# Key tiles of 128 rows by way of HBM, and the last 32 keys' value matmuls in four row groups of the TensorE

One core of one Trainium2 chip. The metric is device time in microseconds (us), the median of several executions; lower is better.

## The reference

A conformer block over `x` of shape (2, 4000, 512): a feed-forward, attention without masking over the 4000 tokens of each batch, a convolution module, a second feed-forward and a layer norm. The part that matters here is the attention, with one head of width 512:

```python
h = _layernorm(x1, axis=-1)
q = h @ w_q
k = h @ w_k
v = h @ w_v
scores = jnp.einsum('btd,bsd->bts', q, k) * scale
p = _softmax(scores, axis=-1)
attn = jnp.einsum('bts,bsd->btd', p, v) @ w_o
x2 = x1 + attn
```

## The kernel before

The kernel folds `w_q` with `w_k` and `w_v` with `w_o`, so keys and values are both the normalized tokens `h`. It keeps a batch's `h` in SBUF twice: `h[kt]` with keys on partitions, for the value matmuls, and `hT` with features on partitions, for the scores. 4000 keys are 32 tiles of 125, each padded with three zero rows. The first batch's tiles are written by the layer norm in SBUF and transposed from there; the second batch's go through HBM and come back tile by tile while the last group of the first batch works.

There are 16 groups of 500 queries. A group runs through all 32 key tiles; per tile it has four score matmuls into one S bank (a bank is a 128x512 buffer in PSUM, where matmuls write), an exponential on ScalarE (ACT) into `P`, an addition to the denominator on VectorE (DVE), and four value matmuls into the four Y banks, which gather over all tiles. Value matmuls come four tiles after their scores. So a group's last value matmuls come behind the fourth score block of the *next* group.

```python
# attention (shortened)
for kt in range(TB):                       # TB = 32 tiles of 125 keys
    ...
    for cc in range(DC):
        self.mm(ps[:, 0:CHUNK], self.hT[kc][:, kj, cc, :], self.qT[s][:, cc, :],
                cc == 0, cc == DC - 1 and not self.any_score, ...)
    self.act(self.P[p], ps[:, 0:CHUNK], AF.Exp, [b_ps], [self.b_P[p]], scale=SCALE)
    ...                                    # acc += P on DVE
    def values(kt=kt, p=p, g=g):
        for dc in range(DC):
            self.mm(self.Yb[dc][:, 0:CHUNK], self.h[kt][:, dc * 128:(dc + 1) * 128], self.P[p],
                    kt == 0, kt == TB - 1, ...)
        if kt == TB - 1:
            self.finish_queries(g, done)   # copies Y0..Y3 out: ACT takes 0 and 2, DVE 1 and 3
    self.lags.append(values)
    if g == 0 and kt < LAG:
        ...
    elif len(self.lags) > LAG:             # LAG = 4
        self.pop(1)
    ...
    hook(g, kt)   # among others: for groups 3 to 16, eight convolution matmuls at kt == 3 and at kt == 8
```

Of the kernel before, what the change touches and what calls it, by code (L numbers as in the profile page):

```python
# [6 lines left out]
BF16 = mybir.dt.bfloat16  # L7
I32 = mybir.dt.int32
ALU = mybir.AluOpType
AF = mybir.ActivationFunctionType  # L10
AX = mybir.AxisListType

B, T, D, F, KW = 2, 4000, 512, 2048, 3
TILE = 125
CHUNK = 500
# [5 lines left out]
TB = T // TILE  # L21
# [197 lines left out]
class Conformer:  # L219
# [19 lines left out]
    def memory(self):  # L239
# [7 lines left out]

        A = Region(nc, "keys", 65536)
        self.h = [A.view(k * 1024, D) for k in range(TB)]
        self.b_h = [A.buf("h%d" % k, k * 1024, 1024) for k in range(TB)]  # L250
        o = TB * 1024
# [145 lines left out]
        self.m3 = C.view(oLT + 4096, CHUNK, parts=3)  # L397
        self.b_m3 = [C.buf("m3", oLT + 4096 + j * 250, 250) for j in range(TPC)]
# [17 lines left out]
        self.keys2 = nc.dram_tensor("keys2", [TB * 128, D], BF16, kind="Internal").ap()  # L416
        self.b_keys2 = [Buf("keys2") for _ in range(TCB)]
# [46 lines left out]
    def mm(self, out, lhsT, rhs, start, stop, reads, bank, inc=None):  # L464
        self.S.op("PE", lambda e: e.matmul(out, lhsT, rhs, start=start, stop=stop),  # L465
                  reads=reads, writes=[bank], inc=stop if inc is None else inc)
# [110 lines left out]
    def ln_job(self, c, at, kind, eng="DVE", gap=1, slot=None):  # L577

        sl = self.nxt("ln", self.LN_SLOTS)

        def tile(ti):
            if kind == "key2":
                self.ln_norm(c, sl, ti, self.h2[ti][0:TILE, :], self.b_h2[ti], eng)
                if ti == TPC - 1:
                    k = c % TCB
                    dst = self.keys2[k * 512:(k + 1) * 512, :].rearrange("(t p) d -> p t d", p=128)
                    self.store(dst, self.h2c, self.b_h2, [self.b_keys2[k]])
                return
            if kind == "key":
                k = c % TCB  # L590
                tok, b_tok = self.h[k * TPC + ti], self.b_h[k * TPC + ti]
                feat, b_feat = self.hT[k][:, ti], self.b_hT[k][ti]
            else:
                s = slot if slot is not None else c % 2
                tok, b_tok = self.ltm[ti], self.b_ltm[ti]
                feat, b_feat = self.lnT[s][:, ti], self.b_lnT[s][ti]
            self.ln_norm(c, sl, ti, tok[0:TILE, :], b_tok, eng)
            self.transpose(feat, tok, [b_tok], [b_feat])

        t = at  # L600
        for ti in range(TPC):
            self.after(t, lambda ti=ti: self.ln_stats(c, sl, ti))
            if ti % 2:
                t += gap
        self.after(t, lambda: self.ln_aggr(c, sl, eng == "ACT"))
        t += 2 * gap
        for ti in range(TPC):
            self.after(t, lambda ti=ti: tile(ti))
            if ti % 2:
                t += gap  # L610
        return t
# [65 lines left out]

    def residual(self, ps, b_ps, g, scalar, b_scalar=()):

        self.S.op("DVE", lambda e: e.scalar_tensor_tensor(  # L680
            out=self.XT[g], in0=ps, scalar=scalar, in1=self.XT[g], op0=ALU.mult, op1=ALU.add),
            reads=[b_ps, self.bx[g]] + list(b_scalar), writes=[self.bx[g]])
# [71 lines left out]
    def q_group(self, b, qc, dc):  # L754

        s = qc % 2
        ps, b_ps = self.sbank()
        out = ps[:, 0:CHUNK].rearrange("p (t k) -> p t k", t=TPC)
        for cc in range(DC):
            self.mm(out, self.M[:, cc, dc * 128:(dc + 1) * 128], self.hT[qc][:, :, cc, 0:TILE],  # L760
                    cc == 0, cc == DC - 1, [self.b_M] + self.b_hT[qc], b_ps)
        if dc % 2:
            self.S.op("DVE", lambda e: e.tensor_copy(self.qT[s][:, dc, :], ps[:, 0:CHUNK]),  # L763
                      reads=[b_ps], writes=[self.b_qT[s][dc]])
        else:
            self.act(self.qT[s][:, dc, :], ps[:, 0:CHUNK], AF.Copy, [b_ps], [self.b_qT[s][dc]])

    def row_max(self, qc):

        S, s = self.S, qc % 2  # L770
        for ti in range(TPC):
            for kc in range(TCB):
                ps, b_ps = self.sbank()
                out = ps[0:TILE, 0:CHUNK].rearrange("p (t k) -> p t k", t=TPC)
                for cc in range(DC):
                    self.mm(out, self.qT[s][:, cc, ti * TILE:(ti + 1) * TILE], self.hT[kc][:, :, cc, 0:TILE],
                            cc == 0, cc == DC - 1, [self.b_qT[s][cc]] + self.b_hT[kc], b_ps)
                S.op("DVE", lambda e, ps=ps, kc=kc: e.tensor_reduce(
                    self.mx[:, kc:kc + 1], ps[0:TILE, 0:CHUNK], AX.X, ALU.max),
                    reads=[b_ps], writes=[self.b_mx[kc]])  # L780
# [22 lines left out]
    def attention(self, old, hook, done):  # L803
        S = self.S
        LAG = 4
        for g in range(NCK):
            b, qc = divmod(g, TCB)
            s = qc % 2
            if self.any_score:
                if qc == 0:  # L810
                    self.pop(len(self.lags))
                    if b:
                        for kt in range(TB):
                            self.second_keys(kt)
                        for dc in range(DC):
                            self.q_group(1, 0, dc)
                self.row_max(qc)
            for kt in range(TB):
                kc, kj = divmod(kt, TPC)
                ps, b_ps = self.sbank()  # L820
                p = self.nxt("P", self.NP)
# [8 lines left out]
                if kt == 0:  # L830
                    S.op("DVE", lambda e, p=p: e.tensor_copy(self.acc[s], self.P[p]),
                         reads=[self.b_P[p]], writes=[self.b_acc[s]])
                else:
                    S.op("DVE", lambda e, p=p: e.tensor_tensor(  # L834
                        out=self.acc[s], in0=self.acc[s], in1=self.P[p], op=ALU.add),
                        reads=[self.b_P[p], self.b_acc[s]], writes=[self.b_acc[s]])

                if kt == TB - 1:
                    self.split_sums(s)
                    if g < NCK - 1:  # L840
                        self.sums_by_query(s)

                def values(kt=kt, p=p, g=g):
                    for dc in range(DC):
                        self.mm(self.Yb[dc][:, 0:CHUNK], self.h[kt][:, dc * 128:(dc + 1) * 128], self.P[p],
                                kt == 0, kt == TB - 1, [self.b_h[kt], self.b_P[p]], self.b_Y[dc],
                                inc=kt == TB - 1 or dc == DC - 1)
                    if kt == TB - 1:
                        self.finish_queries(g, done)
# [6 lines left out]
                if g + 1 < NCK and kt in (14, 16, 18, 20) and not (self.any_score and g + 1 == TCB):  # L856
                    self.q_group((g + 1) // TCB, (g + 1) % TCB, (kt - 14) // 2)
                if not self.any_score:
                    if g == TCB - 1 and kt >= 6:
                        self.second_keys(kt - 6)  # L860
                    if g == TCB and kt < 6:
                        self.second_keys(TB - 6 + kt)
# [3 lines left out]
    def second_keys(self, kt):  # L866

        kc, kj = divmod(kt, TPC)
        src = self.keys2[kt * 128:(kt + 1) * 128, :]
        self.load(self.h[kt], src, [self.b_h[kt]], reads=[self.b_keys2[kc]])  # L870
        self.transpose(self.hT[kc][:, kj], src, [self.b_keys2[kc]], [self.b_hT[kc][kj]])
# [10 lines left out]
    def sums_by_query(self, s):  # L882
# [5 lines left out]
        def reduce():  # L888
            S.op("DVE", lambda e: e.tensor_reduce(
                self.sq[s], self.sT[0:TILE, :, :, 0:TILE].rearrange("p h c k -> p c h k"), AX.XY, ALU.add),  # L890
# [278 lines left out]
    def constants(self):  # L1169
# [4 lines left out]
        for j in range(TPC):  # L1174
# [6 lines left out]

        S.op("POOL", lambda e: e.memset(self.onec, 1.0), writes=[self.b_onec])
        S.op("POOL", lambda e: e.affine_select(
            out=self.onec, in_=self.onec, pattern=[[0, 2]], compare_op=ALU.is_ge, fill=0.0,
            base=TILE - 1, channel_multiplier=-1), reads=[self.b_onec], writes=[self.b_onec])
        S.op("POOL", lambda e: e.memset(self.one3, 0.0), writes=[self.b_one3])
        S.op("POOL", lambda e: e.memset(self.one3[:, 0:TILE], 1.0), reads=[self.b_one3], writes=[self.b_one3])

    def zero_keys(self, kc):
        for k in range(kc * TPC, (kc + 1) * TPC):  # L1190
            self.S.op("POOL", lambda e, k=k: e.memset(self.h[k], 0.0), writes=[self.b_h[k]])


    def program(self, any_score):
# [26 lines left out]
        def ff1(c, old):  # L1221
            def hook(f):
# [4 lines left out]
                if c < TCB and f == 6:  # L1227
                    self.zero_keys(c)
# [5 lines left out]
                if c == TCB - 1 and f < TPC:  # L1234
                    self.S.op("POOL", lambda e: e.memset(self.h2[f], 0.0), writes=[self.b_h2[f]])

            self.ff_chunk(c, old, hook, lambda: self.ln_job(c, 5, "key" if c < TCB else "key2"))
# [225 lines left out]
```

## Time and profile before

| | before |
|---|---|
| median, 4 runs | 2060.54 us (2060.18 to 2060.61) |
| span in the trace | 2056.5 us |
| TensorE (PE) busy | 2044.2 us, 9653 matmuls |
| DVE, ACT, GpSimd (POOL) busy | 1110, 744, 129 us |
| DMA engines, queue 1 | 17.4% of the span |

PE is the bound. Since its busy time is modelled from pipelined matmuls, read the *starts* of matmuls and not their lengths.

### The profile page before, as it was taken

How to read it: one execution, taken by the hardware profiler on the slowest of the kernel's cores; microseconds unless marked ns; L12 is line 12 of the kernel's file. 1: busy time of each engine (PE TensorE's matmuls, PEld its weight loads, DVE VectorE, ACT ScalarE, POOL GpSimd, SP SyncE). 2: the span in 40 equal slices, each digit the busy share in tenths (PEclk: the TensorE clock that was granted, in tenths of full speed). 3: DMA queues.
4: the chain of work that ended last, by engine and by line, in shares of the span. 5: the costliest groups of instructions: out<-in, count | busy, mean ns of one | idle time of the engine just before them, and what ended most of it. 6: DMA issues, size and time to landing. Idle time of an engine off the chain costs nothing.

```text
span 2056.5 us, 24392 instructions
## 1 busy us (share of the span) xinstructions
PE 2044.2 (99%) x9653; PEld 1037.7 (50%) x9653; DVE 1110.0 (54%) x2274; ACT 744.3 (36%) x1270; POOL 128.7 (6%) x275
## 2 busy tenths in 40 slices
PE   9999999999999999999999999999999999999998
PEld 5555555554444444444444444444445555555554
DVE  4244444325556667666666676667764443443443
ACT  3433333333333333333333333333345443443432
POOL 2012100000000000000000000000011000000000
PEclk9999999999999999999999999999999999999999
DMA  7232221110001100114301010101143111111111
GB/s 181 54 62 57 56 61 49 46 49 11 16 6 24 24 16 18 21 23 110 92 17 24 18 24 14 23 18 24 38 129 93 31 31 41 31 31 41 31 31 42
DMA packets 209324, 87.73 MB, mean 43 GB/s; under 512 B 157873, under 2 KB 208692, under 8 KB 209204
## 3 DMA queue, kind: packets, MB, share of 16 engines
q1 hardware_dynamic: 208808, 85.79, 17.4%
q8 instruction: 78, 1.28, 0.3%
q14 instruction: 42, 0.34, 0.1%
q10 hardware_dynamic: 396, 0.31, 0.0%
HBM read 29.53 MB, written 19.04 MB: 24 GB/s over the span
## 4 chain that ended last, share of the span: by engine, by line
PE 98%; DVE 1%; issue 0%; POOL 0%; DMA 0%; SPq 0%; ACT 0%; POOLq 0%; DVEq 0%; ACTq 0%
PE s L465 55%; PE y L465 42%; DVE wff L1062 0%; DVE work L547 0%; DMA wff<-in_w_ff_a_dram 0%; DVE xt L680 0%; SPq L519 0%; DVE work L569 0%; POOL work L674 0%; POOL work L1071 0%; DVE wff L967 0%; DVE work L504 0%; ACT work L507 0%; PE y L493 0%; DVE work L1069 0%
## 5 line engine op out<-in xcount | busy, mean ns | idle before, releaser
L507 ACT ACTIVATE work<-s 128x500 bf16<-128x500 f32 (+1 forms) x1060 | 621.6, 587 | 1219.8 <-PE s L465 1218.2
L465 PE MATMUL s<-work,wff 128*128 128x500 bf16 (+2 forms) x2592 | 628.3, 373 | 2.5 <-DVE work L504 1.7
L465 PE MATMUL s<-work,keys 128*128 128x500 bf16 x2048 | 517.5, 374 | 0.1
L465 PE MATMUL y<-work,keys 128*128 128x500 bf16 x2048 | 514.4, 373 | 0.1
L465 PE MATMUL y<-wff,work 128*125 128x512 bf16 x2016 | 506.6, 379 | 0.0
L834 DVE TENSOR_TENSOR work<-work 128x500 f32<-128x500 f32 x496 | 334.4, 674 | 282.1 <-ACT work L507 279.2
L465 PEld LDWEIGHTS s<-work,wff 128*128 128x128 bf16 x2592 | 251.9, 98 | 280.3 <-issue 2.1
L465 PEld LDWEIGHTS y<-wff,work 128*125 128x125 bf16 x2016 | 275.2, 137 | 173.5
L465 PEld LDWEIGHTS y<-work,keys 128*128 128x128 bf16 x2048 | 199.2, 97 | 234.4 <-DVE work L899 1.1
L465 PEld LDWEIGHTS s<-work,keys 128*128 128x128 bf16 x2048 | 199.8, 98 | 232.2 <-DVE work L763 0.6
L680 DVE SCALAR_TENSOR_TENSOR xt<-y,xt 125x512 bf16<-125x512 f32 x128 | 79.7, 683 | 343.8 <-PE y L465 343.8
L547 DVE BATCH_NORM_STATS2 work<-xt 125x6 f32<-125x512 bf16 x316 | 199.7, 680 | 7.9 <-DMA xt<-in_x_dram 7.7
L556 POOL TENSOR_TENSOR work<-work 125x4 f32<-125x4 f32 x76 | 77.0, 1013 | 1115.2 <-DVE work L554 1115.2
L465 PE MATMUL s<-work 128*125 128x512 bf16 (+3 forms) x524 | 133.5, 379 | 2.1 <-DVE work L1172 1.3
L569 DVE TENSOR_SCALAR work<-xt,work 125x512 bf16<-125x512 bf16 x279 | 111.7, 444 | 16.8 <-POOL work L556 13.0
L680 DVE SCALAR_TENSOR_TENSOR xt<-s,xt 125x512 bf16<-125x512 f32 x56 | 38.7, 692 | 146.4 <-PE s L465 146.4
L465 PEld LDWEIGHTS s<-work 128*125 128x125 bf16 (+2 forms) x524 | 70.3, 136 | 47.9 <-issue 3.5
L680 DVE SCALAR_TENSOR_TENSOR xt<-s,work,xt 125x512 bf16<-125x512 f32 x64 | 48.0, 751 | 32.6 <-PE s L465 32.0
L465 PE MATMUL s<-keys,work 128*128 128x500 bf16 x256 | 64.4, 376 | 0.0
L971 DVE SCALAR_TENSOR_TENSOR wff<-wff,s 128x500 bf16<-128x500 f32 x57 | 38.6, 678 | 43.5 <-PE s L465 41.5
L507 ACT ACTIVATE wff<-s 128x500 f32<-128x500 f32 x67 | 39.2, 586 | 57.2 <-PE s L465 55.2
L507 ACT ACTIVATE work<-keys,work 128x500 bf16<-128x500 bf16 x64 | 50.4, 794 | 1.1 <-DVE work L1076 1.1
(89 smaller groups left out, 493.8 us busy)
## 6 DMA issues: line engine op xcount, KB each, us to landing
xt<-in_x_dram SPq DMA_DIRECT2D x15, 500.0 KB
out_dram<-work SPq DMA_DIRECT2D x15, 500.0 KB
dcvd<-wff SPq DMA_DIRECT2D x52, 125.0 KB, 1.7
keys<-dcvd SPq DMA_DIRECT2D x13, 500.0 KB, 4.4
wff<-in_w_ff_a_dram SPq DMA_DIRECT2D x16, 256.0 KB, 4.4
keys<-work SPq DMA_DIRECT2D x8, 512.0 KB, 3.6
keys<-keys SPq DMA_DIRECT2D x32, 128.0 KB, 2.1
work<-work SPq DMA_TRANSPOSE x210, 2.5
```

The source lines that it names most:

```text
L465: self.S.op("PE", lambda e: e.matmul(out, lhsT, rhs, start=start, stop=stop), reads=reads, writes=[bank], inc=stop if inc is None else inc)
L507: return self.S.op("ACT", lambda e: e.activation(out, in_, func, **kw), reads=reads, writes=writes)
L547: self.S.op("DVE", lambda e: e.bn_stats(self.st[sl][:, ti, :], x), reads=[b_x], writes=[self.b_st[sl][ti]])
L556: S.op("POOL", lambda e: e.tensor_tensor(out=self.rs[sl], in0=self.va[sl], in1=self.neghalf[0:TILE, :], op=ALU.pow), reads=self.b_va[sl] + ...
L569: self.S.op("DVE", lambda e: e.tensor_scalar(out, x, self.mv[sl][:, ti, 0:1], self.rs[sl][:, ti:ti + 1], ALU.subtract, ALU.mult), reads=[b ...
L680: self.S.op("DVE", lambda e: e.scalar_tensor_tensor(out=self.XT[g], in0=ps, scalar=scalar, in1=self.XT[g], op0=ALU.mult, op1=ALU.add), rea ...
L834: S.op("DVE", lambda e, p=p: e.tensor_tensor(out=self.acc[s], in0=self.acc[s], in1=self.P[p], op=ALU.add), reads=[self.b_P[p], self.b_acc[ ...
L971: self.S.op("DVE", lambda e: e.scalar_tensor_tensor(out=out, in0=self.th[k], scalar=1.0, in1=ps[:, 0:CHUNK], op0=ALU.add, op1=ALU.mult), r ...
```

## The change

Its intent: cut the keys into 31 tiles of 128 and one of 32, and use the array that the small tile leaves idle. The 32 keys are stored four times in the last tile, so that scores and exponentials come out in four copies, one in each quarter of the partitions. The four value matmuls of that tile then take one copy each, on four different row groups of the array and into four different banks, and can run at once. Tiles of 128 don't fit the chunks of 125 x 4 tokens in which the layer norm makes them, so both batches now go through HBM, and the queries, which used to be read from `hT`, get their own transposes. The core of the diff, shortened:

```diff
-TB = T // TILE
+KT = -(-T // 128)
+REST = T % 128
...
+    def store_keys(self, c):                      # 500 rows to HBM; at a batch's end also the tail, four times
...
+            S.dma("SP", k, *[lambda e, r=r: e.dma_start(self.tailsd[b, r:r + REST, :],
+                                                        self.h2[TPC - 1][TILE - REST:TILE, :])
+                             for r in range(0, 128, REST)], ...)
...
+    def fetch_queries(self, b, qc, ti):
+        self.transpose(self.lnT[sl][:, ti], self.keysd[b, t0:t0 + 128, :], ...)
...
                 def values(kt=kt, p=p, g=g):
                     for dc in range(DC):
-                        self.mm(self.Yb[dc][:, 0:CHUNK], self.h[kt][:, dc * 128:(dc + 1) * 128], self.P[p],
-                                kt == 0, kt == TB - 1, [self.b_h[kt], self.b_P[p]], self.b_Y[dc],
-                                inc=kt == TB - 1 or dc == DC - 1)
+                        r = slice(dc * REST, (dc + 1) * REST) if kt == KT - 1 else slice(0, 128)
+                        self.mm(self.Yb[dc][:, 0:CHUNK], self.h[kt][r, dc * 128:(dc + 1) * 128], self.P[p][r],
+                                kt == 0, kt == KT - 1, [self.b_h[kt], self.b_P[p]], self.b_Y[dc],
+                                inc=kt == KT - 1 or dc == DC - 1,
+                                **({"tile_position": (dc * REST, 0)} if kt == KT - 1 else {}))
...
+                if g + 1 < NCK and 7 <= kt < 7 + TPC:
+                    self.fetch_queries((g + 1) // TCB, (g + 1) % TCB, kt - 7)
...
+                if c > TCB and f >= 2 and f % 2 == 0:        # first batch's keys, during chunks 9 to 13
+                    k = (c - TCB - 1) * 7 + f // 2 - 1
+                    if k < KT:
+                        self.key_tile(0, k)
...
-    def zero_keys(self, kc):
```

More of the change, by code (lines that the diff above doesn't have):

```diff
@@ L248, in memory @@
         A = Region(nc, "keys", 65536)
-        self.h = [A.view(k * 1024, D) for k in range(TB)]
-        self.b_h = [A.buf("h%d" % k, k * 1024, 1024) for k in range(TB)]
-        o = TB * 1024
+        self.h = [A.view(k * 1024, D) for k in range(KT)]
+        self.b_h = [A.buf("h%d" % k, k * 1024, 1024) for k in range(KT)]
+        o = KT * 1024
         self.hT = [A.view(o + t * 4096, 2048).rearrange("p (t c k) -> p t c k", t=TPC, c=DC)
@@ L396, in memory @@
         self.b_one3 = Buf("one3")
-        self.m3 = C.view(oLT + 4096, CHUNK, parts=3)
-        self.b_m3 = [C.buf("m3", oLT + 4096 + j * 250, 250) for j in range(TPC)]
+        self.m3 = C.view(oP + (self.NP - 1) * 1024, CHUNK, parts=3)
+        self.b_m3 = [C.buf("m3", oP + (self.NP - 1) * 1024 + j * 250, 250) for j in range(TPC)]
         self.hl = C.view(oHL, 1024).rearrange("p (h c k) -> p h c k", h=2, c=DC)
@@ L415, in memory @@
         self.b_Y = [Buf("y%d" % i, excl=True) for i in range(4)]
-        self.keys2 = nc.dram_tensor("keys2", [TB * 128, D], BF16, kind="Internal").ap()
-        self.b_keys2 = [Buf("keys2") for _ in range(TCB)]
+        self.keysd = nc.dram_tensor("keysd", [B, KT * 128, D], BF16, kind="Internal").ap()
+        self.b_keysd = [Buf("keysd") for _ in range(NCK)]
+        self.tailsd = nc.dram_tensor("tailsd", [B, 128, D], BF16, kind="Internal").ap()
+        self.b_tailsd = [Buf("tailsd") for _ in range(B)]
         self.dcvd = nc.dram_tensor("dcvd", [self.NBESIDE, 128, DC * CHUNK], BF16, kind="Internal").ap()
@@ L461, in drain, with mm @@
             self.tick()
-    def mm(self, out, lhsT, rhs, start, stop, reads, bank, inc=None):
-        self.S.op("PE", lambda e: e.matmul(out, lhsT, rhs, start=start, stop=stop),
+    def mm(self, out, lhsT, rhs, start, stop, reads, bank, inc=None, **kw):
+        self.S.op("PE", lambda e: e.matmul(out, lhsT, rhs, start=start, stop=stop, **kw),
                   reads=reads, writes=[bank], inc=stop if inc is None else inc)
@@ L581, in tile @@
         def tile(ti):
-            if kind == "key2":
+            if kind == "key":
                 self.ln_norm(c, sl, ti, self.h2[ti][0:TILE, :], self.b_h2[ti], eng)
                 if ti == TPC - 1:
-                    k = c % TCB
-                    dst = self.keys2[k * 512:(k + 1) * 512, :].rearrange("(t p) d -> p t d", p=128)
-                    self.store(dst, self.h2c, self.b_h2, [self.b_keys2[k]])
+                    self.store_keys(c)
                 return
-            if kind == "key":
-                k = c % TCB
-                tok, b_tok = self.h[k * TPC + ti], self.b_h[k * TPC + ti]
-                feat, b_feat = self.hT[k][:, ti], self.b_hT[k][ti]
-            else:
-                s = slot if slot is not None else c % 2
-                tok, b_tok = self.ltm[ti], self.b_ltm[ti]
-                feat, b_feat = self.lnT[s][:, ti], self.b_lnT[s][ti]
+            s = slot if slot is not None else c % 2
+            tok, b_tok = self.ltm[ti], self.b_ltm[ti]
+            feat, b_feat = self.lnT[s][:, ti], self.b_lnT[s][ti]
             self.ln_norm(c, sl, ti, tok[0:TILE, :], b_tok, eng)
@@ L676, in ln_factor @@
              reads=[self.b_va[sl][ti], self.b_neghalf], writes=[self.b_rs[sl][ti]])
+    def store_keys(self, c):
+        b, qc = divmod(c, TCB)
+        S, dst = self.S, self.keysd[b, qc * CHUNK:(qc + 1) * CHUNK, :].rearrange("(t p) d -> p t d", p=TILE)
+        k = S.dsems[36 + self.nxt("st", 8)]
+        S.dma("SP", k, *[lambda e, lo=lo, hi=hi: e.dma_start(dst[lo:hi], self.h2c[lo:hi]) for lo, hi in self.ROWS],
+              reads=self.b_h2, writes=[self.b_keysd[c]])
+        if qc == TCB - 1:
+            n = 128 - TILE
+            self.store(self.keysd[b, T:T + n, :], self.h2[TPC - 1][TILE:128, :], [self.b_h2[TPC - 1]],
+                       [self.b_keysd[c]])
+            k = S.dsems[36 + self.nxt("st", 8)]
+            S.dma("SP", k, *[lambda e, r=r: e.dma_start(self.tailsd[b, r:r + REST, :],
+                                                        self.h2[TPC - 1][TILE - REST:TILE, :])
+                             for r in range(0, 128, REST)],
+                  reads=[self.b_h2[TPC - 1]], writes=[self.b_tailsd[b]])
     def residual(self, ps, b_ps, g, scalar, b_scalar=()):
@@ L754, in q_group @@
     def q_group(self, b, qc, dc):
-        s = qc % 2
+        s, sl = qc % 2, 1 if b or qc else 0
         ps, b_ps = self.sbank()
@@ L759, in q_group @@
         for cc in range(DC):
-            self.mm(out, self.M[:, cc, dc * 128:(dc + 1) * 128], self.hT[qc][:, :, cc, 0:TILE],
-                    cc == 0, cc == DC - 1, [self.b_M] + self.b_hT[qc], b_ps)
+            self.mm(out, self.M[:, cc, dc * 128:(dc + 1) * 128], self.lnT[sl][:, :, cc, 0:TILE],
+                    cc == 0, cc == DC - 1, [self.b_M] + self.b_lnT[sl], b_ps)
         if dc % 2:
@@ L766, in q_group @@
             self.act(self.qT[s][:, dc, :], ps[:, 0:CHUNK], AF.Copy, [b_ps], [self.b_qT[s][dc]])
+    def fetch_queries(self, b, qc, ti):
+        sl, t0 = 1 if b or qc else 0, qc * CHUNK + ti * TILE
+        self.transpose(self.lnT[sl][:, ti], self.keysd[b, t0:t0 + 128, :],
+                       self.b_keysd[b * TCB + qc:b * TCB + min(qc + 2, TCB)], [self.b_lnT[sl][ti]])
     def row_max(self, qc):
@@ L773, in row_max @@
                 ps, b_ps = self.sbank()
-                out = ps[0:TILE, 0:CHUNK].rearrange("p (t k) -> p t k", t=TPC)
+                out = ps[0:TILE, :].rearrange("p (t k) -> p t k", t=TPC)
                 for cc in range(DC):
-                    self.mm(out, self.qT[s][:, cc, ti * TILE:(ti + 1) * TILE], self.hT[kc][:, :, cc, 0:TILE],
+                    self.mm(out, self.qT[s][:, cc, ti * TILE:(ti + 1) * TILE], self.hT[kc][:, :, cc, :],
                             cc == 0, cc == DC - 1, [self.b_qT[s][cc]] + self.b_hT[kc], b_ps)
                 S.op("DVE", lambda e, ps=ps, kc=kc: e.tensor_reduce(
-                    self.mx[:, kc:kc + 1], ps[0:TILE, 0:CHUNK], AX.X, ALU.max),
+                    self.mx[:, kc:kc + 1], ps[0:TILE, :], AX.X, ALU.max),
                     reads=[b_ps], writes=[self.b_mx[kc]])
@@ L812, in attention @@
                     if b:
-                        for kt in range(TB):
-                            self.second_keys(kt)
-                        for dc in range(DC):
-                            self.q_group(1, 0, dc)
+                        for kt in range(KT):
+                            self.key_tile(1, kt)
                 self.row_max(qc)
-            for kt in range(TB):
+            for kt in range(KT):
                 kc, kj = divmod(kt, TPC)
                 ps, b_ps = self.sbank()
-                p = self.nxt("P", self.NP)
+                p = self.nxt("Pa", self.NP - 1) if self.any_score else self.nxt("P", self.NP)
                 for cc in range(DC):
@@ L833, in attention @@
                 else:
-                    S.op("DVE", lambda e, p=p: e.tensor_tensor(
-                        out=self.acc[s], in0=self.acc[s], in1=self.P[p], op=ALU.add),
+                    n = REST if kt == KT - 1 else 128
+                    acc = self.acc[s][0:n]
+                    S.op("DVE", lambda e, p=p, n=n, acc=acc: e.tensor_tensor(
+                        out=acc, in0=acc, in1=self.P[p][0:n], op=ALU.add),
                         reads=[self.b_P[p], self.b_acc[s]], writes=[self.b_acc[s]])
-                if kt == TB - 1:
+                if kt == KT - 1:
                     self.split_sums(s)
@@ L844, in values @@
                     for dc in range(DC):
-                        self.mm(self.Yb[dc][:, 0:CHUNK], self.h[kt][:, dc * 128:(dc + 1) * 128], self.P[p],
-                                kt == 0, kt == TB - 1, [self.b_h[kt], self.b_P[p]], self.b_Y[dc],
-                                inc=kt == TB - 1 or dc == DC - 1)
-                    if kt == TB - 1:
+                        r = slice(dc * REST, (dc + 1) * REST) if kt == KT - 1 else slice(0, 128)
[3 more added lines that the diff above has]
+                                **({"tile_position": (dc * REST, 0)} if kt == KT - 1 else {}))
+                    if kt == KT - 1:
                         self.finish_queries(g, done)
@@ L855, in attention @@
                     self.pop(1)
-                if g + 1 < NCK and kt in (14, 16, 18, 20) and not (self.any_score and g + 1 == TCB):
+                if g + 1 < NCK and 7 <= kt < 7 + TPC:
+                    self.fetch_queries((g + 1) // TCB, (g + 1) % TCB, kt - 7)
+                if g + 1 < NCK and kt in (14, 16, 18, 20):
                     self.q_group((g + 1) // TCB, (g + 1) % TCB, (kt - 14) // 2)
@@ L859, in attention, with key_tile @@
                     if g == TCB - 1 and kt >= 6:
-                        self.second_keys(kt - 6)
+                        self.key_tile(1, kt - 6)
                     if g == TCB and kt < 6:
-                        self.second_keys(TB - 6 + kt)
+                        self.key_tile(1, KT - 6 + kt)
                 hook(g, kt)
                 self.tick()
-    def second_keys(self, kt):
+    def key_tile(self, b, kt):
         kc, kj = divmod(kt, TPC)
-        src = self.keys2[kt * 128:(kt + 1) * 128, :]
-        self.load(self.h[kt], src, [self.b_h[kt]], reads=[self.b_keys2[kc]])
-        self.transpose(self.hT[kc][:, kj], src, [self.b_keys2[kc]], [self.b_hT[kc][kj]])
+        if kt == KT - 1:
+            src, rd = self.tailsd[b], [self.b_tailsd[b]]
+        else:
+            src = self.keysd[b, kt * 128:(kt + 1) * 128, :]
+            lo, hi = kt * 128 // CHUNK, (kt * 128 + 127) // CHUNK
+            rd = self.b_keysd[b * TCB + lo:b * TCB + hi + 1]
+        self.load(self.h[kt], src, [self.b_h[kt]], reads=rd)
+        self.transpose(self.hT[kc][:, kj], src, rd, [self.b_hT[kc][kj]])
     def split_sums(self, s):
@@ L889, in reduce @@
             S.op("DVE", lambda e: e.tensor_reduce(
-                self.sq[s], self.sT[0:TILE, :, :, 0:TILE].rearrange("p h c k -> p c h k"), AX.XY, ALU.add),
+                self.sq[s], self.sT[0:TILE].rearrange("p h c k -> p c h k"), AX.XY, ALU.add),
                 reads=self.b_sT, writes=[self.b_sq[s]])
@@ L1182, in constants @@
         S.op("POOL", lambda e: e.memset(self.onec, 1.0), writes=[self.b_onec])
-        S.op("POOL", lambda e: e.affine_select(
-            out=self.onec, in_=self.onec, pattern=[[0, 2]], compare_op=ALU.is_ge, fill=0.0,
-            base=TILE - 1, channel_multiplier=-1), reads=[self.b_onec], writes=[self.b_onec])
-        S.op("POOL", lambda e: e.memset(self.one3, 0.0), writes=[self.b_one3])
-        S.op("POOL", lambda e: e.memset(self.one3[:, 0:TILE], 1.0), reads=[self.b_one3], writes=[self.b_one3])
-    def zero_keys(self, kc):
-        for k in range(kc * TPC, (kc + 1) * TPC):
-            self.S.op("POOL", lambda e, k=k: e.memset(self.h[k], 0.0), writes=[self.b_h[k]])
+        S.op("POOL", lambda e: e.memset(self.one3, 1.0), writes=[self.b_one3])
     def program(self, any_score):
@@ L1226, in hook @@
                     self.ln_job(c + 1, 1, "in")
-                if c < TCB and f == 6:
-                    self.zero_keys(c)
                 if c == 0 and f == 8:
@@ L1233, in hook @@
                     self.after(6, self.taps)
-                if c == TCB - 1 and f < TPC:
+                if c > TCB and f >= 2 and f % 2 == 0:
+                    k = (c - TCB - 1) * 7 + f // 2 - 1
+                    if k < KT:
+                        self.key_tile(0, k)
+                if c == NCK - 1 and f >= FC - TPC:
+                    self.fetch_queries(0, 0, f - FC + TPC)
+                if c == 0 and f < TPC:
                     self.S.op("POOL", lambda e: e.memset(self.h2[f], 0.0), writes=[self.b_h2[f]])
-            self.ff_chunk(c, old, hook, lambda: self.ln_job(c, 5, "key" if c < TCB else "key2"))
+            self.ff_chunk(c, old, hook, lambda: self.ln_job(c, 5, "key"))
         old = 0
```

## The prediction

> **What bounds the kernel now.** I read the page first: busy time, then the chain that ended last.
>
> ```profile
> span 2056.5 us, 24392 instructions
> PE 2044.2 (99%) x9653; PEld 1037.7 (50%) x9653; DVE 1110.0 (54%) x2274; ACT 744.3 (36%) x1270; POOL 128.7 (6%) x275
> ...
> PE 98%; DVE 1%; issue 0%; POOL 0%; DMA 0%; SPq 0%; ACT 0%; POOLq 0%; DVEq 0%; ACTq 0%
> ```
>
> The TensorE is 99% busy and 98% of the chain. A busy PE can hide gaps, so next comes the timeline, in the middle of one attention group (500 queries against all keys of a batch). Columns: start in us, length in us, engine, line, operation, how many merged.
>
> ```profile
> 500.40 1.01 PE L465 MATMUL s<-work,keys 128*128 128x500 bf16 x4
> ...
> 501.25 1.00 PE L465 MATMUL y<-work,keys 128*128 128x500 bf16 x4
> ```
>
> Four matmuls start every 0.845 us, so one 500-wide matmul costs 0.845 / 4 = 0.211 us. 9653 x 0.212 = 2046 us, which is the PE's busy time: there is no slack between matmuls in general, and time is the count of matmuls times their spacing. Only two things can move the end: fewer or overlapping matmuls, and new gaps between them. DVE at 54%, ACT at 36% and DMA at a tenth or two matter only where PE waits for them.
>
> **What the Trainium skill says.** (1) "Perfetto Trace Analysis", Tensor Engine Instruction: a matmul's end in the trace is estimated, not observed. The trace agrees: a matmul is shown 0.374 us long, yet starts are 0.211 us apart. I use starts alone. (2) "TensorE: Matmul & The Clock Gate", Part 3: four matmuls of 32 contraction rows in four row groups run at the same time, starts about 4 ns apart, 3.07x measured for 512 columns. No run here shows it yet. (3) "TensorEngine Tiling (Array Packing)", Key Properties: changing the tiling mode drains the TensorE, changing only the tile does not. This the trace of before does show, in an unexpected place: the tap weights are turned by four matmuls of 3 contraction rows, and the score bound by a matmul with one output row; as built, both are instructions for a part of the array (32 rows by 128 columns; 128 by 32), like the new ones. Here they are between full matmuls, and below them, for control, eight matmuls one column wide that stay on the whole array:
>
> ```profile
> 45.13 1.03 PE L465 MATMUL y<-wff,work 128*125 128x512 bf16 x4
> 46.09 0.25 PE L465 MATMUL s<-work 3*128 3x3 bf16 x4
> 46.28 1.02 PE L465 MATMUL s<-work,wff 128*128 128x500 bf16 x4
> ...
> 93.46 1.03 PE L465 MATMUL y<-wff,work 128*125 128x512 bf16 x4
> 94.42 0.19 PE L465 MATMUL s<-work 128*1 128x1 f32 x2
> 94.54 1.02 PE L465 MATMUL s<-work,wff 128*128 128x500 bf16 x4
> ...
> 1524.30 0.80 PE L465 MATMUL y<-work,keys 128*128 128x500 bf16 x3
> 1524.93 0.58 PE L465 MATMUL s<-work 128*125 128x1 bf16 x8
> 1525.37 1.00 PE L465 MATMUL y<-work,keys 128*128 128x500 bf16 x4
> ```
>
> A merged line ends when its last matmul ends, so the last one started at start + length - one matmul's length (0.379 us for 512 columns, 0.374 for 500, 0.163 for 3, 0.164 for 1x1). Into the small mode: 45.13 + 1.03 - 0.38 = 45.78, next start 46.09, 0.31 us; and 93.46 + 1.03 - 0.38 = 94.11, next 94.42, again 0.31. A 512-wide matmul normally holds its successor for 0.216, so the switch costs about 0.095 us. The control: 1524.30 + 0.80 - 0.37 = 1524.73, next 1524.93, 0.20, no penalty. Back out: 46.09 + 0.25 - 0.16 = 46.18, next 46.28; 94.42 + 0.19 - 0.16 = 94.45, next 94.54: 0.09 to 0.10 after a matmul with almost no columns of its own. So I charge 0.095 us per switch, each way. The four 3-row matmuls started (46.18 - 46.09) / 3 = 0.03 us apart.
>
> **The change, part by part.** *The tiles.* Before, 4000 keys are 32 tiles of 125; after, 31 of 128 and one of 32. The count stays 32, so score matmuls (4 per tile), the exponentials and the sums of the denominator keep their number and, but for one addition of 32 rows, their size. Nothing is gained there.
>
> *The last value tile.* This is the whole gain. Its four 128-row matmuls become four 32-row ones on separate rows of the array and separate banks. From the start of the full matmul before them to the start of the full one after them: before, 5 x 0.211 = 1.057 us. After: 0.211 + 0.095 to enter, 3 x 0.03 to start the other three (I take the spacing that this trace shows, not the page's 4 ns), 0.211 for the last to stream, 0.095 to leave: 0.702 us. Saving: 0.355 us for each of 16 query groups, if nothing else stops PE.
>
> *Where something else does.* The four value banks must be copied out before the next group's first value matmuls overwrite them. Shorter matmuls come to that point sooner; the copies do not, since they queue on ACT and DVE behind an exponential and an addition of the new group, whose start depends on its fourth score block and not on the value matmuls. The boundary between the first and second group:
>
> ```profile
> 520.69 1.01 PE L465 MATMUL s<-work,keys 128*128 128x500 bf16 x4
> ...
> 521.32 1.25 DVE L899 CAST work<-y 128x500 bf16<-128x500 f32 x2
> 521.54 1.48 PE L465 MATMUL y<-work,keys 128*128 128x500 bf16 x4
> ...
> 522.63 0.10 PEld L465 LDWEIGHTS y<-work,keys 128*128 128x128 bf16 x1 [0.47 <-DVE work L899]
> ```
>
> The four value matmuls take 1.48 us in place of 1.00: PE already waits for the DVE copies, which end at 522.57. The last cannot start before 522.63 however soon PE arrives, so here the saving is lost: 0. The same boundary between later groups:
>
> ```profile
> 721.07 1.86 PE L465 MATMUL s<-work,wff 128*128 128x500 bf16 x8
> ...
> 721.64 1.26 DVE L899 CAST work<-y 128x500 bf16<-128x500 f32 x2
> ...
> 722.77 1.01 PE L465 MATMUL s<-work,keys 128*128 128x500 bf16 x4
> ...
> 723.62 1.00 PE L465 MATMUL y<-work,keys 128*128 128x500 bf16 x4
> ```
>
> From the third group on, eight matmuls of the convolution stand in between. The copies end at 722.90 and the first value matmul comes at 723.62, the fourth at 724.25. Moved up 0.355 us they start at 723.27 and 723.90: still no wait. After the last group there are also eight such matmuls before the projection reads the copies. So 15 of 16 groups keep it: 15 x 0.355 = 5.3 us.
>
> *The way through HBM.* Now both batches' keys are stored, loaded and transposed from HBM; before, only the second's. Added: 32 more loads of 128 KB, 32 more key transposes in place of 32 from SBUF, 64 transposes for the queries, and small stores for the tail. The view of DMA issues (KB each, median us to landing) has the same operations:
>
> ```profile
> keys<-keys SPq DMA_DIRECT2D x32, 128.0 KB, 2.1
> ...
> keys<-keys SPq DMA_TRANSPOSE x64, 2.7
> ```
>
> The first batch's keys are issued over chunks 9 to 13 of the first feed-forward, whose chunks last 27.4 us, and used after chunk 15. The queries are fetched at key tiles 7 to 10 and used at 14; the last has four tiles of 1.69 us, 6.8 us, against 2.7. The second batch's keys keep their place. The tail stores after the last chunk follow its normalization (ends 476.4), and the copy that overwrites their source comes at about 482.8 (it follows the query matmuls that start at 481.78): 6 us for seven small transfers against one of 2 to 4 us. Cost on PE: 0. *GpSimd* loses 32 clearings of key tiles; it is 6% busy, so 0.
>
> Sum: 2060.5 - 5.3 = 2055.2 us.
>
> **Rivals.** (a) *No drain worth the name*: the pack takes what the skill's 3.07x gives, 4 x 0.211 / 3.07 = 0.275 us (an estimate from that page's ratio); 15 x (0.845 - 0.275) = 8.5 us, 2052.0. Against it: 0.095 us measured at both small-mode places. With the page's 4 ns between starts but the drain as measured, 0.355 + 3 x 0.026 = 0.43 us, 6.5 us in all, 2054.0. (b) *Weights in the open*: weight loads (0.097 us each, of the value tiles) are not hidden in the pack, and the starts are 0.1 us apart; the saving is 0.634 - 0.19 - 0.3 = 0.14 us, 2.2 us in all, 2058.4. For it: the loads of the 3-row matmuls began only with them, at 46.09, not one matmul early as elsewhere. Against: those started 0.03 us apart. (c) *The four do not overlap at all*: two switches are then pure loss, 16 x 0.19 = 3 us, 2063.5. (d) *A late transfer*: one of the fetches or the tail stores holds PE at a group's query matmuls. Each wait of 1 us in 15 groups would be 15 us, 2070; the margins of 4 us speak against it. (e) The copies become the limit at every boundary, as at the first: gain 0, 2060.5. The eight convolution matmuls speak against it.
>
> **Range and chances.** (a) and (b) bracket what I believe: 2052.5 to 2060.0 leaves room for part of (e) on the upper side. Faster by over 2% would need 41 us; all value matmuls of the last tiles together are 16 x 0.845 = 13.5 us: 1%. Slower by over 2% needs waits of 2.8 us in every group: 2%.
>
> **What would show it.** In the timeline of after, at the end of a group: the last full score matmul, 0.31 us later the first 32-row one, three more within 0.1 us, and the next full one 0.3 us after the last. The boundary of the first two groups: value matmuls stretched by about 0.8 in place of 0.48 us, waiting on the DVE copy; from the third on no such wait. PE's waits naming DMA: none in attention. The prediction is wrong if the 32-row starts lie 0.1 or 0.2 us apart, if the switch costs clearly more or less than 0.095 us, or if a wait on a transfer appears ahead of the query or score matmuls.

## The result, and the profile after

The changed kernel takes 2054.41 us (4 runs, 2054.03 to 2054.93), against 2060.54: 6.1 us less. The ratio is 0.9971, 95% interval 0.9954 to 0.9988. Ratios here are the mean time of one kernel's fast runs over that of the other's of the same rounds, so not quite the ratio of the medians quoted. The point predicted was 2055.2, the range 2052.5 to 2060.0.

The page of after, its span and busy times; below it, from the view by shape, the group of the new matmuls (count, busy us, mean ns of one, idle before). PEld is the loading of weights for PE, SPq below the issuing of transfers:

```profile
span 2050.2 us, 24503 instructions
PE 2037.8 (99%) x9653; PEld 1031.8 (50%) x9653; DVE 1099.0 (54%) x2274; ACT 742.7 (36%) x1270; POOL 112.2 (5%) x241
```

```profile
L470 PE MATMUL y<-work,keys 32*128 32x500 bf16 x64 | 6.2, 380 | 0.0
```

PE still executes 9653 matmuls; it is busy for 6.4 us less because 64 of them overlap. Busy time can show overlap; a count cannot. The end of the second group, in the timeline of before and then of after:

```profile
583.84 1.01 PE L465 MATMUL s<-work,keys 128*128 128x500 bf16 x4
...
584.69 1.00 PE L465 MATMUL y<-work,keys 128*128 128x500 bf16 x4
...
585.53 1.86 PE L465 MATMUL s<-work,wff 128*128 128x500 bf16 x8
```

```profile
583.65 1.01 PE L470 MATMUL s<-work,keys 128*128 128x500 bf16 x4
584.59 0.10 PEld L470 LDWEIGHTS y<-work,keys 32*128 32x128 bf16 x4 [0.41 <-issue]
584.60 0.39 PE L470 MATMUL y<-work,keys 32*128 32x500 bf16 x4
...
584.92 1.87 PE L470 MATMUL s<-work,wff 128*128 128x500 bf16 x8
...
585.92 1.25 DVE L929 CAST work<-y 128x500 bf16<-128x500 f32 x2
...
587.48 1.00 PE L470 MATMUL y<-work,keys 128*128 128x500 bf16 x4
```

The last full matmul before the pack starts at 583.65 + 1.01 - 0.37 = 584.29. The pack starts 0.31 us later, as at the tap weights. The four matmuls together last 0.39 us where one lasts 0.38: they start within 0.01 us. The next full matmul comes at 584.92, 0.32 us after the pack's start. From full to full 584.92 - 584.29 = 0.63 us, against 5 x 0.211 = 1.06 before (585.53 - 584.48 in its lines): 0.43 us saved. The DVE copies end at 587.17, and the next value matmuls start at 587.48 without a wait.

The boundary of the first two groups, again before and then after:

```profile
519.00 1.01 PE L465 MATMUL s<-work,keys 128*128 128x500 bf16 x4
...
522.86 1.01 PE L465 MATMUL s<-work,keys 128*128 128x500 bf16 x4
```

```profile
518.81 1.01 PE L470 MATMUL s<-work,keys 128*128 128x500 bf16 x4
...
519.75 0.39 PE L470 MATMUL y<-work,keys 32*128 32x500 bf16 x4
...
520.08 1.02 PE L470 MATMUL s<-work,keys 128*128 128x500 bf16 x4
...
521.04 0.38 PE L470 MATMUL y<-work,keys 128*128 128x500 bf16 x1
521.13 1.26 DVE L929 CAST work<-y 128x500 bf16<-128x500 f32 x2
...
521.86 0.97 PE L470 MATMUL y<-work,keys 128*128 128x500 bf16 x3 [0.44 <-DVE work L929]
...
522.67 1.01 PE L470 MATMUL s<-work,keys 128*128 128x500 bf16 x4
```

The first score block after the stalled value matmuls starts at 522.67; the fourth score block of this group starts at 518.81. That is 3.86 us. Before, the same two starts are at 519.00 and 522.86: also 3.86. This boundary kept nothing. Its value matmuls are stretched by 522.67 - 521.04 - 0.845 = 0.79 us, as forecast (about 0.8).

### The profile page after: what moved, and what is told of

Read it like the earlier page. It is cut to its first block, busy times and chain, and to the rows that moved or that the text cites. A ratio compares the mean times of both kernels' runs of the same rounds, so it can differ in the third digit from the quotient of the medians.

```text
span 2050.2 us, 24503 instructions
## 1 busy us (share of the span) xinstructions
PE 2037.8 (99%) x9653; PEld 1031.8 (50%) x9653; DVE 1099.0 (54%) x2274; ACT 742.7 (36%) x1270; POOL 112.2 (5%) x241
## 4 chain that ended last, share of the span: by engine, by line
PE 98%; DVE 1%; POOL 0%; issue 0%; ACT 0%; DMA 0%; POOLq 0%; SPq 0%; DVEq 0%; ACTq 0%
PE s L470 55%; PE y L470 42%; DVE work L552 0%; POOL work L672 0%; DVE work L574 0%; DVE wff L1092 0%; DVE xt L695 0%; DMA xt<-in_x_dram 0%; DVE work L509 0%; POOL work L1101 0%; DVE work L665 0%; ACT work L512 0%; DVE wff L997 0%; DVE work L618 0%; DVE work L670 0%
## 5 line engine op out<-in xcount | busy, mean ns | idle before, releaser
L470 PE MATMUL y<-work,keys 128*128 128x500 bf16 (+1 forms) x2048 | 504.6, 374 | 0.4 <-DVE work L929 0.4
L854 DVE TENSOR_TENSOR work<-work 128x500 f32<-128x500 f32 (+1 forms) x496 | 334.4, 674 | 280.0 <-ACT work L512 277.2
L470 PEld LDWEIGHTS y<-work,keys 128*128 128x128 bf16 (+1 forms) x2048 | 194.6, 97 | 234.0 <-issue 6.2
L470 PE MATMUL s<-work 128*125 128x512 bf16 (+2 forms) x780 | 197.7, 378 | 2.0 <-DVE work L1202 1.2
L470 PEld LDWEIGHTS s<-work 128*125 128x125 bf16 (+1 forms) x780 | 95.3, 124 | 76.9 <-issue 3.7
L1071 POOL COPY wff<-wff 128x1 bf16<-128x1 bf16 x56 | 10.5, 187 | 635.4 <-DVE wff L1001 633.0
```

What stands on the lines that cost most here:

```text
L470: self.S.op("PE", lambda e: e.matmul(out, lhsT, rhs, start=start, stop=stop, **kw), reads=reads, writes=[bank], inc=stop if inc is None el ...
L854: S.op("DVE", lambda e, p=p, n=n, acc=acc: e.tensor_tensor(out=acc, in0=acc, in1=self.P[p][0:n], op=ALU.add), reads=[self.b_P[p], self.b_a ...
L1071: S.op("POOL", lambda e: e.tensor_copy(self.G[gs][:, jj, 0:1], self.G[gp][:, jj, CHUNK:CHUNK + 1]), reads=[self.b_G[gp][jj]], writes=[self ...
```

## Experiments

Four kernels ran in each of two calls, each call on one chip; the kernel before took 2060.58 us (9 runs) in the first and 2060.28 us (7 runs) in the second. All eight gave the right result.

**after_again**: the changed kernel, no edit, beside the next three.

> The changed kernel as it is, for its size beside the next three on one chip. Theory (15 boundaries keep 0.42 us each, the trace's value, the first keeps none): 6.3 us under the kernel before, ratio 0.9969. Rival (part of the gain is from elsewhere, such as the way through HBM): the same ratio here, told apart by the next two.

Measured: 2054.70 us (5 runs, 2054.15 to 2054.75), ratio 0.9971, interval 0.9957 to 0.9984. The gain is there on this chip too, 5.9 us by medians.

**hbm_only**: HBM and tiles of 128 without the row groups.

```diff
-                        r = slice(dc * REST, (dc + 1) * REST) if kt == KT - 1 else slice(0, 128)
+                        r = slice(0, 128)
...
-                                inc=kt == KT - 1 or dc == DC - 1,
-                                **({"tile_position": (dc * REST, 0)} if kt == KT - 1 else {}))
+                                inc=kt == KT - 1 or dc == DC - 1)
...
+        if kt == KT - 1:
+            for r in range(REST, 128, REST):
+                self.after(12, lambda r=r: self.S.op("DVE", lambda e: e.memset(self.h[kt][r:r + REST], 0.0), ...))
```

> Tiles of 128 by way of HBM, but the last tile's rows 32 to 127 are cleared and its value matmuls are four of 128 rows, one after the other, as before. Theory: all of the gain is the row groups, so this equals the kernel before, within 0.5 us (ratio 1.000). Rival: the way through HBM or the dropped clearings of GpSimd give something by themselves, and this is 1 us or more faster; or it costs something that the row groups cover, and it is 1 us or more slower.

Measured: 2060.94 us (5 runs, 2060.74 to 2061.22), ratio 1.0002, interval 0.9988 to 1.0015. The medians differ by 0.36 us, and the runs of the kernel before alone spread over 1.4: tiling and transfers together change the time by less than the runs scatter. No part of the gain is theirs, so it lies in the four matmuls per group. Their trace does show one small price, 0.38 us of waiting on a transfer (see (d) below).

**serial_rows**: the two mode switches without work side by side.

```diff
-                        r = slice(dc * REST, (dc + 1) * REST) if kt == KT - 1 else slice(0, 128)
+                        r = slice(0, REST) if kt == KT - 1 else slice(0, 128)
...
-                                **({"tile_position": (dc * REST, 0)} if kt == KT - 1 else {}))
+                                **({"tile_position": (0, 0)} if kt == KT - 1 else {}))
```

> The last tile's four value matmuls keep 32 contraction rows but all use rows 0 to 31, so the same two mode switches without work side by side. Theory: four starts 0.21 us apart between two switches of 0.1 us; 15 x 0.2 us = 3 us over the kernel before, 9.4 us over the changed one (about 2063.6). Rival 1 (the gain is from fewer rows per matmul, not from running at once): as fast as the changed kernel, 2054.4. Rival 2 (weights of one row group can't be loaded while it works): starts 0.31 us apart, about 2069.

Measured: 2063.67 us (4 runs, 2063.54 to 2064.28), ratio 1.0015, interval 1.0000 to 1.0031. Its timeline at the end of the second group:

```profile
583.74 1.01 PE L470 MATMUL s<-work,keys 128*128 128x500 bf16 x4
584.67 0.53 PEld L470 LDWEIGHTS y<-work,keys 32*128 32x128 bf16 x4 [0.41 <-issue]
584.68 1.01 PE L470 MATMUL y<-work,keys 32*128 32x500 bf16 x4
585.62 1.88 PE L470 MATMUL s<-work,wff 128*128 128x500 bf16 x8
```

Four matmuls on one row group last 1.01 us, (1.01 - 0.37) / 3 = 0.21 us from start to start, exactly as full ones: a quarter of the contraction rows saves nothing. The weights are loaded beside a running matmul of the same row group: the last load starts at 584.67 + 0.53 - 0.10 = 585.10, the last matmul only at 584.68 + 1.01 - 0.37 = 585.32. From full to full: 583.74 + 1.01 - 0.37 = 584.38 to 585.62, 1.24 us, 0.19 more than without switches. Running at once is the gain; the switches are its price. Both rivals fall.

**late_first**: the first boundary freed from the copies.

```diff
-                elif len(self.lags) > LAG:
-                    self.pop(1)
+                elif len(self.lags) > LAG and not (g == 1 and kt == 4):
+                    self.pop(2 if g == 1 and kt == 10 else 1)
```

> The changed kernel, but in the second group the first value tile is issued one score block later, so that the copies out of the value banks are over by then; the extra tile of lag is made up at tile 10. Theory (this boundary lost its 0.42 us and the 0.48 us that it already waited to the DVE copies): 0.8 us under the changed kernel, about 2053.6, and no PE wait on the copies there. Rival (PE would wait for something else in that place, or the copies only come later too): no difference, 2054.4.

Measured: 2053.51 us (5 runs, 2053.30 to 2054.26), ratio 0.9965, interval 0.9951 to 0.9979. By medians that is 1.2 us under the changed kernel of the same call, of which 0.8 was expected. The profiled run is the slowest, 2054.26; the other four end by 2053.52. The timeline shows the place itself:

```profile
520.17 1.87 PE L470 MATMUL s<-work,keys 128*128 128x500 bf16 x8
...
521.23 1.25 DVE L929 CAST work<-y 128x500 bf16<-128x500 f32 x2
...
521.88 1.05 PE L470 MATMUL y<-work,keys 128*128 128x500 bf16 x4
...
522.76 1.01 PE L470 MATMUL s<-work,keys 128*128 128x500 bf16 x4
```

Two score blocks run while the copies work, and the value matmuls take 1.05 us in place of 1.00, where the changed kernel stretched them over 522.67 - 521.04 = 1.63 us. From the pack's start (519.85 here, 519.75 in the changed kernel) 2.91 us pass until the next score block in both; but here two score blocks and the value matmuls are done by then, there only one and the value matmuls. One block is 0.845 us. Two waits of weight loads on the copies are left (0.19 and 0.35 us), but cost only the 0.05 by which the value matmuls are longer. Up to the second pack the whole block is kept, first after_again, then late_first:

```profile
519.85 0.39 PE L470 MATMUL y<-work,keys 32*128 32x500 bf16 x4
...
584.69 0.39 PE L470 MATMUL y<-work,keys 32*128 32x500 bf16 x4
```

```profile
519.85 0.39 PE L470 MATMUL y<-work,keys 32*128 32x500 bf16 x4
...
583.85 0.39 PE L470 MATMUL y<-work,keys 32*128 32x500 bf16 x4
```

That is 0.84 us, so the theory holds. The profiled run lost as much again at another place, to a transfer; see (d) below. What the medians differ by beyond this, 0.4 us, is not explained. This version has the lowest median of all.

**switch48 and noswitch48**: the switch by itself. Ahead of three score blocks of each group, one matmul of three columns, whose output the block overwrites; with 32 rows in the first, with 128 in the second (`0:128` in place of `0:32`).

```diff
+                if kt in (11, 13, 25) and not self.any_score:
+                    self.mm(ps[:, 0:3], self.ident[0:32, :], self.ident[0:32, 0:3], True, True, [self.b_ident], b_ps, inc=False)
                 for cc in range(DC):
```

> The changed kernel with one matmul of 32 rows and 3 columns put in ahead of three score blocks of each group (48 in all), so two mode switches each and hardly any work. Theory (0.1 us per switch): 48 x 0.2 = 9.6 us over the changed kernel, about 2064. Rival (the switch is nearly free, and the 0.31 us at the tap weights and at the pack is a wait on something else): under 3 us over the changed kernel.

> The control: the same 48 matmuls of 3 columns with all 128 rows, so no switch. Theory: 0.03 to 0.055 us each, as the one-column matmuls of the kernel before, 1.5 to 2.6 us over the changed kernel, about 2056.5. Rival (any narrow matmul among wide ones costs 0.2 us): as slow as the version with switches.

Measured: 2064.42 us (4 runs, 2064.34 to 2064.91) and 2055.29 us (4 runs, 2055.06 to 2055.74), on the same chip. Timelines, switch48 first, at the first such place of the second group (the fifth of the x5 is the added matmul):

```profile
535.20 1.13 PE L470 MATMUL s<-work 128*125 128x512 bf16 x5
536.26 1.02 PE L470 MATMUL s<-work,keys 128*128 128x500 bf16 x4
```

```profile
534.71 1.03 PE L470 MATMUL s<-work 128*125 128x512 bf16 x5
535.60 1.01 PE L470 MATMUL s<-work,keys 128*128 128x500 bf16 x4
```

Four 512-wide matmuls hold PE for 4 x 0.216 = 0.864 us. With the small matmul in another mode the next block starts after 1.06 us, with the same matmul on the whole array after 0.89. Over all, (2064.42 - 2055.29) / 48 = 0.19 us for two switches. The rival that called 0.31 us a wait on something else falls: the same matmul without a switch has no such gap. The control itself cost less than expected: 0.6 us over the changed kernel, not 1.5 to 2.6. It was run at another time.

**moved_before and moved_after**: the eight convolution matmuls taken from between the last and the first value matmuls of neighbouring groups, in both kernels.

```diff
-            if 0 <= g - 2 < tail and kt in (3, 8):
-                pair(g - 2, 2 + (3, 8).index(kt))
+            if 0 <= g - 2 < tail and kt in (4, 8):
+                pair(g - 2, 2 + (4, 8).index(kt))
```

> The kernel before, with the convolution's eight matmuls at the head of groups 3 to 16 one key tile later, behind the first value tile and not in front of it. Theory: each of these 14 boundaries now waits as the first does, 0.48 us; 6.7 us over the kernel before, about 2067. Rival (the copies have slack without them): no change.

> The same move in the changed kernel. Theory: at these boundaries the pack's gain is lost to the copies, as at the first one, so it is nearly as slow as the kernel before with the move: 0.4 us less (only the last group keeps its gain), about 2066.8. Rival (the gain of the pack doesn't depend on what stands behind it): 6.3 us under the kernel before with the move, about 2061.

Measured: 2066.19 us (4 runs, 2066.06 to 2066.39) and 2065.95 us (4 runs, 2065.83 to 2066.21). The change that is worth 6 us in the original order is worth 0.24 us in this one, and both are slower than the kernel before. The waits of PE's weight loads on the DVE copies (us in total, times, longest), first moved_before, then moved_after, then the changed kernel:

```profile
PEld y L465 <- DVE work L899: 15.5, 30, 0.6
```

```profile
PEld y L470 <- DVE work L929: 17.9, 30, 0.7
```

```profile
PEld y L470 <- DVE work L929: 1.2, 2, 0.7
```

Two waits at one boundary have become 30 at 15. The row groups make PE arrive sooner at banks that come free no sooner. The move cost the kernel before 5.9 us, 0.42 per boundary and not 0.48. (The waits in the table total more than what they cost: a weight load normally starts 0.21 us ahead of its matmul.)

## Why the prediction was right

- *PE alone sets the end.* Held: with everything but the row groups in place (hbm_only) the time is that of the kernel before, although the DMA queue's share rose from 17.4% to 21.5% and GpSimd lost 16.5 us of work.
- *The switch costs 0.095 us each way.* Held, and well beyond the two places it was read from: 0.19 us per pair in switch48 against its control, 0.19 in serial_rows. That it could be read from the kernel before, at four forgotten matmuls of 3 rows, is what made the estimate possible.
- *The other three matmuls start 0.03 us apart.* This term was mis-sized. The trace of after has (0.39 - 0.38) / 3 = 0.003 us (its records, finer than these lines, have starts 3 to 4 ns apart). The 3-row matmuls from which 0.03 was taken all use rows 0 to 2 of the array, so one row group; the 4 ns of the Trainium skill ("TensorE: Matmul & The Clock Gate", Part 3) for different row groups was the better value, as the prediction's second estimate under rival (a) had it (0.43 us per group, 2054.0). That one group is the reason for 0.03 is likely, and was not tested by itself; the control noswitch48 fits, where a matmul of 3 columns on all 128 rows also holds PE for 0.89 - 0.864 = 0.03 us.
- *15 of 16 boundaries keep it.* Held. 15 x 0.43 = 6.4 us, against 6.3 us between the two spans and 6.1 us between the medians. The first boundary kept 0.00 us. That the copies are what decides is shown from both sides: late_first frees that boundary, the moved pair takes the gain from the others.
- *Rivals.* (b), weights in the open, is out: weight loads do start only with the pack (PEld idle 0.41 us before them), but the starts are not 0.1 us apart. What the 0.095 us consist of, a drain of the array or these loads in the open (0.10 us each), no run here separates. (c), no overlap, is out by the trace, and its 2063.5 is what serial_rows measured when overlap was made impossible: 2063.67. (e) is the state that moved_after built.
- *(d), a late transfer.* The prediction put the cost of the transfers on PE at 0 and expected no wait on a DMA in attention. That is slightly off. The fetches that it named never hold the query matmuls. But at one place of the eighth group, while the second batch's keys come in, eight convolution matmuls start late. The kernel before, then late_first:

```profile
965.90 1.01 PE L465 MATMUL y<-work,keys 128*128 128x500 bf16 x4
966.75 1.86 PE L465 MATMUL s<-work,wff 128*128 128x500 bf16 x8
```

```profile
962.47 1.00 PE L470 MATMUL y<-work,keys 128*128 128x500 bf16 x4
964.15 1.86 PE L470 MATMUL s<-work,wff 128*128 128x500 bf16 x8 [0.68 <-DMA work<-work]
```

  From the last value matmul's start, 0.21 us pass before the change and 1.05 in late_first, 0.84 too many. It is 0.07 in the trace of after, 0.32 in after_again and 0.38 in hbm_only. The wait named is on transposes (`work<-work`). That the added transfers push these back in the same queue is likely, and was not tested.

  The margin of the tail stores was misread. The prediction gave seven stores 6 us until a copy overwrites their source. In after, the last four are issued at 480.2 to 481.4 and land about 1.6 us later (the view of their line, then the timeline):

```profile
L688 SPq DMA_DIRECT2D tailsd<-work x4: 324/417/421, 480.2 to 481.4; - x4
DMA to landing us min/median/max: 1.5/1.6/1.6
```

```profile
476.22 0.84 SPq L680 DMA_DIRECT2D keysd<-work  x2
...
480.15 1.71 SPq L688 DMA_DIRECT2D tailsd<-work  x4
...
482.70 0.59 ACT L512 ACTIVATE work<-s 128x500 bf16<-128x500 f32 x1 [1.11 <-PE s L470]
...
495.44 0.68 DVE L778 CAST work<-s 128x500 bf16<-128x500 f32 x1 [0.49 <-PE s L470]
```

  So the stores take from 476.2 to 481.4 + 1.6 = 483.0, 6.8 us, longer than the margin and past the copy at 482.70 that the prediction had in mind. Nothing waited, because that copy overwrites only the buffer's first 1000 bytes, which the large store reads. The tail's source lies in bytes 3072 to 4096 (`h2[3]`; `qT[1]` begins at the same address), and only the fourth query copy reaches it, at 495.44. Here the prediction was right by luck.

  The other transfers took what the same operations took before: key loads 2.3 us against 2.1, key transposes 2.8 against 2.7.

## What to carry to other kernels

Packing small matmuls into row groups is worth (n - 1) matmuls less two mode switches, so count the switches first: here they took 0.19 of the 0.42 us of a pack, and a pack of two would, as an estimate from these numbers, have gained almost nothing (0.21 - 0.19). Then ask what stands right behind the pack: the same banks must be emptied before their next use, PE now gets there sooner, and only other work in between turns the saved time into an earlier end. To price something new, look for a small relative of it in the trace that you have.

## What the Trainium skill lacked or had wrong

- "TensorEngine Tiling (Array Packing)", Key Properties, says that a change of tiling mode drains the TensorE, without a cost. Here: 0.095 us per switch, 0.19 us in and out (switch48 less its control, 48 pairs, 9.1 us), and weight loads of the new mode are not issued ahead of it (PEld idle for 0.41 us before the pack's loads).
- "TensorE: Matmul & The Clock Gate", Part 3: starts about 4 ns apart agree (0.003 us). Its 3.07x for four row tiles does not carry over to a pack within a stream of full matmuls: 0.845 us became 0.63 - 0.21 = 0.42 us, twice as fast. Without the 0.19 of the switches, which that part does not mention, it would be 0.23 (an estimate).
- "TensorEngine Tiling (Array Packing)", PSUM Bottleneck, says that copies out of PSUM may become the limit after a speedup, and gives no size. Without other matmuls in between, 6 us of gain shrink to 0.24.
